# Attention scores on quarters of the matmul array, with the masked quarter of each tile left out

## The chip, the cores and the metric

One NeuronCore of a Trainium2 chip runs the whole program. The metric is the device time of one execution in microseconds (us), as a median over runs. TensorE (PE in the rows) does the matmuls and PEld is its weight load; VectorE (DVE), ScalarE (ACT) and GpSimd (POOL) work on elements; SyncE (SP) only issues DMA transfers.

## The reference, cut to what matters

```
scores = q @ k.T / sqrt(64)                     # batch 8, heads 8, seq 576, head_dim 64
D      = gamma[h] ** (i - j) where i >= j, else 0
attn   = (scores * D) @ v                       # -> x[4608, 512]
e      = argmax(x @ w_gate + modality_bias)     # one of 8 experts for each token
x      = gate * (relu(x @ w1[e]) @ w2[e])       # 512 -> 1024 -> 512
h      = x @ w_in                               # 512 -> 2048
out    = (h - tanh(h)) @ w_out                  # -> [4608, 512]
```

Only the first part, the attention with decay (a retention layer), is touched by the change. A score counts only where the key's position j is not after the query's position i.

## The kernel before, in words

The 4608 tokens of all eight batches stand in one row and are cut into 36 tiles of 128 tokens (`TL`, `NTILE`). A sequence has 576 tokens, which is 4.5 tiles, so the pattern of the sequences repeats every 9 tiles (`PERIOD`), and in every tile t with t % 9 == 4 one sequence ends and the next begins in the middle; the kernel calls it the mid tile. The decay is split into a factor for the query's position (`gx`, applied after the product with v) and one for the key's position (`vsc`, applied to v). What remains on the scores is a mask of ones and zeros.

The eight heads are four pairs p, each with two heads s = 0, 1. The work on a tile, by function:

- `scores(t)`: for each p and s one matmul of the 64 rows of head s (rows 0 to 63 or 64 to 127 of the array), all 128 columns (the key tokens) and 128 streamed query tokens, into a PSUM tile `sc` for each s (line 304). Two VectorE instructions of 128x512 elements then multiply `sc` by the mask into `a` (line 308). There are three `sc` buffers.
- `scaled(t)`: GpSimd makes `vs` = v times `vsc` (line 314).
- `attend(t)`: three groups of eight matmuls. `before()` adds what earlier tiles of the sequence give, from a running state: quarters of the array, 64 rows and 64 columns, 128 streamed tokens, or 64 in a mid tile (line 340). Line 348 adds the product of `a` and `vs`: 128 rows, halves of the columns. Line 363 brings the state forward from k and `vs`: 128 rows and halves of the columns, or in the mid tile the lower 64 rows alone. ScalarE copies the state to SBUF (line 367).
- `evac_x(t)`: VectorE multiplies the result `xp` by `gx` into `xt` (line 373). There is a single `xp` buffer, so the next tile's lines 340 and 348 wait for it.

The loop runs one tile ahead with the scores. Each pass t issues scores(t+1), attend(t), evac_x(t), scaled(t+4) and the loads of tile t+6. With every fourth tile the routing of a group of four tiles is woven in: `route_a` (line 404), `route_b` (transposes on line 413 and a chain of small VectorE instructions, lines 417 to 429) and `route_c` (small matmuls on lines 438 to 443, and a chain on lines 446 to 456). Each pass also transposes an older tile (line 471), which ScalarE scales by the gate and stores, and scatters token numbers by GpSimd (line 460). The order on every engine is the order of the program, written by hand. Where t % 9 is 0 there is nothing earlier in the sequence and `before()` does not run; in a mid tile it runs behind line 348; elsewhere it comes first, directly behind the scores of the next tile.

All these matmuls are in full float32, and each of them stands in the trace as two instructions (16 for eight matmuls), each with a weight load of its own.

Behind the attention come the experts (line 642 and lines 836 to 838) and the last two layers (line 642 and lines 910 to 912). The first unit of the experts starts on rows that GpSimd gathers (line 154) once tile 31's scatters have gone out; their transposes are on line 144.

## Time and profile before

| what | value |
|---|---|
| median of 3 runs (lowest to highest) | 1431.66 us (1431.45 to 1434.45) |
| the profiled execution, its own time | 1423.35 us |
| its span, from the first to the last instruction | 1421.6 us |
| granted TensorE clock, mean over the span | 0.994 |
| busy: PE, PEld, DVE, ACT, POOL | 98%, 85%, 73%, 48%, 16% |

The profiled execution is 8.3 us shorter than the median of the runs shown. A busy time is the union of an engine's instructions. Matmuls overlap each other in time, so the time that a group of them takes is read from where it starts to where the next group starts, and not from the durations. In the timeline a row gives the start, the time covered, engine, line, operation, tiles, shape and count; in brackets stands how long the engine had been idle, and what ended that.

### The profile page before, as it was taken

The page shows a single profiled execution, that of the slowest core. Times are in us where ns is not written, and L with a number is a line of the kernel's source. Part 1 is how long each engine was busy: PE and PEld are TensorE (multiplying, and loading weights), DVE is VectorE, ACT ScalarE, POOL GpSimd, SP SyncE. Part 2 cuts the span into 40 slices and gives each one's busy share as a digit, 9 for nine tenths or more (in the row PEclk, how much of TensorE's full clock was granted, in tenths as well). Part 3 has the DMA queues.
Part 4 walks back from the last instruction along what each step waited for, and adds up shares of the span by engine and source line. Part 5 has one row for each costly group of instructions (what it writes and reads, how often), then busy time and mean ns, then how long its engine had stood idle before and what let it go on. Part 6 is the DMA issues. An engine that isn't in the chain of part 4 may idle for free.

```text
span 1421.6 us, 22507 instructions
## 1 busy us (share of the span) xinstructions
PE 1392.0 (98%) x8427; PEld 1210.5 (85%) x8427; DVE 1044.5 (73%) x1761; ACT 682.9 (48%) x1269; POOL 220.8 (16%) x288
## 2 busy tenths in 40 slices
PE   7999999999999999989999999999999999999997
PEld 6888799999999999968888888888888888888885
DVE  3666678888888888557777777787777877778764
ACT  1233444444444444445555555555556555556553
POOL 3655420011111111100011100111001111011101
PEclk9999999999999999999999999999999999999999
DMA  9998533554754446253000000000000000000000
GB/s 355 407 335 304 192 131 124 135 135 136 228 116 79 90 121 162 71 165 127 30 30 30 30 1 30 30 30 30 1 30 30 30 30 0 30 30 1 30 1 30
DMA packets 65682, 138.71 MB, mean 98 GB/s; under 512 B 22480, under 2 KB 29328, under 8 KB 65568
## 3 DMA queue, kind: packets, MB, share of 16 engines
q1 hardware_dynamic: 49360, 96.15, 22.0%
q0 software_dynamic: 7904, 21.96, 4.6%
q10 hardware_dynamic: 8304, 19.11, 3.5%
q8 instruction: 68, 1.11, 0.3%
q14 instruction: 46, 0.38, 0.1%
HBM read 135.16 MB, written 39.80 MB: 123 GB/s over the span
## 4 chain that ended last, share of the span: by engine, by line
PE 50%; issue 5%; DVE 1%; POOL 0%; ACT 0%; POOLq 0%; DVEq 0%; ACTq 0%
PE hp L642 25%; PE acc L910 8%; PE acc L911 8%; PE acc L912 8%; POOL out_dram L935 0%; DVE xh L886 0%; DVE xl L893 0%; ACT xh L884 0%; DVE xl L895 0%; DVE xl L894 0%; DVE lo L889 0%; POOLq L963 0%; DVE xl L885 0%; POOL nopt L934 0%; ACT xh L883 0%
## 5 line engine op out<-in xcount | busy, mean ns | idle before, releaser
L883 ACT ACTIVATE xh<-hp 128x512 f32<-128x512 f32 x144 | 86.1, 598 | 329.9 <-PE hp L642 315.4
L910 PE MATMUL acc<-wout,hi 128*128 128x512 f32 x576 | 225.7, 392 | 5.1 <-ACT xh L883 5.1
L642 PE MATMUL hp<-yh,winh 128*128 128x512 f32 x576 | 226.4, 393 | 1.3 <-DVE epsb L939 1.3
L642 PE MATMUL hp<-yl,winh 128*128 128x512 f32 x576 | 226.2, 393 | 0.0
L642 PE MATMUL hp<-yh,winl 128*128 128x512 f32 x576 | 226.2, 393 | 0.0
L911 PE MATMUL acc<-wout,hi 128*128 128x512 f32 x576 | 225.6, 392 | 0.0
L912 PE MATMUL acc<-wout,lo 128*128 128x512 f32 x576 | 224.7, 390 | 0.0
L885 DVE TENSOR_TENSOR xl<-xh,hp 128x512 f32<-128x512 f32 x144 | 99.0, 687 | 167.7 <-ACT xh L884 167.7
L894 DVE SCALAR_TENSOR_TENSOR xl<-xh,xl 128x512 f32<-128x512 f32 x144 | 128.2, 890 | 15.4 <-DVE xl L893 0.5
L836 PE MATMUL acc<-hi,wh 128*128 128x400 f32 x384 | 136.9, 357 | 0.2
L910 PEld LDWEIGHTS acc<-wout,hi 128*128 128x128 f32 x576 | 108.6, 189 | 29.6 <-ACT xh L883 5.5
L642 PE MATMUL hp<-xl,wh 128*128 128x400 f32 x384 | 133.2, 347 | 0.1
L642 PE MATMUL hp<-xh,wl 128*128 128x400 f32 x384 | 133.0, 346 | 0.0
L642 PE MATMUL hp<-xh,wh 128*128 128x400 f32 x384 | 132.5, 345 | 0.2 <-ACT wh L711 0.2
L838 PE MATMUL acc<-hi,wl 128*128 128x400 f32 x384 | 132.6, 345 | 0.0
L837 PE MATMUL acc<-lo,wh 128*128 128x400 f32 x384 | 131.4, 342 | 0.0
L642 PEld LDWEIGHTS hp<-yh,winh 128*128 128x128 f32 x576 | 108.2, 188 | 25.7 <-PEq L857 1.6
L642 PEld LDWEIGHTS hp<-yh,winl 128*128 128x128 f32 x576 | 108.1, 188 | 24.6
L912 PEld LDWEIGHTS acc<-wout,lo 128*128 128x128 f32 x576 | 108.6, 189 | 23.9 <-DVE lo L889 0.4
L642 PEld LDWEIGHTS hp<-yl,winh 128*128 128x128 f32 x576 | 108.3, 188 | 23.9
L911 PEld LDWEIGHTS acc<-wout,hi 128*128 128x128 f32 x576 | 108.4, 188 | 23.1
L736 ACT ACTIVATE hi<-hp 128x400 fp32r<-128x400 f32 x96 | 48.4, 505 | 164.5 <-PE hp L642 164.5
(162 smaller groups left out, 2517.7 us busy)
## 6 DMA issues: line engine op xcount, KB each, us to landing
raw<-in_w_dram SPq DMA_DIRECT2D x91, 512.0 KB
qk<-in_qk_dram SPq DMA_DIRECT2D x36, 512.0 KB
vk<-in_vk_dram SPq DMA_DIRECT2D x35, 512.0 KB
y_d<-yo SPq DMA_DIRECT2D x12, 800.0 KB
yr<-y_d SPq DMA_DIRECT2D x9, 1024.0 KB
raw<-in_wo_dram SPq DMA_DIRECT2D x16, 512.0 KB
wo_d<-cv_em ACTq DMA_DIRECT2D x16, 512.0 KB
raw<-in_wi_dram SPq DMA_DIRECT2D x16, 512.0 KB
```

The lines of the kernel that those rows point to most:

```text
L642: nc.tensor.matmul(out=hp, lhsT=lhs, rhs=rhs, start=j == 0, stop=j == 3 * KD - 1)
L736: nc.scalar.activation(out=hi, in_=hp, func=ACTF.Relu)
L836: nc.tensor.matmul(out=o, lhsT=wh[:, cs], rhs=hi, start=first, stop=False)
L837: nc.tensor.matmul(out=o, lhsT=wh[:, cs], rhs=lo, start=False, stop=False)
L838: nc.tensor.matmul(out=o, lhsT=wl[:, cs], rhs=hi, start=False, stop=last)
L883: nc.scalar.activation(out=u, in_=hp, func=ACTF.Square)
L885: nc.vector.tensor_tensor(out=v, in0=u, in1=hp, op=ALU.mult)
L894: nc.vector.scalar_tensor_tensor(out=v, in0=s, scalar=SQ_C, in1=v, op0=ALU.add, op1=ALU.mult)
L910: nc.tensor.matmul(out=acc[s], lhsT=hi, rhs=wh, start=first, stop=False)
L911: nc.tensor.matmul(out=acc[s], lhsT=hi, rhs=wl, start=False, stop=False)
L912: nc.tensor.matmul(out=acc[s], lhsT=lo, rhs=wh, start=False, stop=last)
```

## The change

The scores of a pair are computed in quarters. For each p, the 64 key tokens of a half (kh = 0, 1) go to a block of 64 columns, c = kh XOR (p mod 2), so that every second pair has its key tokens swapped by halves. The upper half of the keys can only be seen by the upper half of the queries, so for kh = 1 only 64 query tokens are streamed. The other quarter of `a` is not computed. It is zeroed once at the start, in two `a` tiles that are used in turn. In place of two VectorE instructions for each tile there are six: for each s one of 128x256 elements for the upper queries, and one on each half of the partitions with 128 elements for the lower queries. The host swaps k, v, `vsc` and a second mask in the same way. As the halves of a mid tile then lie in different places for different pairs, its state product runs over all 128 rows, with a second `vs2` that is zero for the tokens of the older sequence.

```diff
 def _consts():
+    mask = np.stack([mask, np.roll(mask, 64, axis=0)], axis=2)
+    vsc = swapped(np.concatenate([vsc, vsc[:, PERIOD // 2:PERIOD // 2 + 1] * (j[:, :, None] >= 64)], axis=1)[None])[0]
...
-            mask = att.tile([128, 2, TL], F32, name="mask")
+            mask = att.tile([128, 2, 2, TL], F32, name="mask")
-            vsc = att.tile([128, PERIOD, H], F32, name="vsc")
+            vsc = att.tile([128, PERIOD + 1, H], F32, name="vsc")
+            weights = [att.tile([128, 2, H // 2, TL], F32, name=f"a{i}") for i in range(2)]
...
+            for a in weights:
+                nc.vector.memset(a, 0.0)
...
             def scores(t):
-                a = tmp.tile([128, 2, H // 2, TL], F32, name="a")
+                a = weights[t % 2]
                 for p in range(H // 2):
-                    for s in range(2):
-                        r64 = slice(64 * s, 64 * s + 64)
-                        nc.tensor.matmul(out=sc[s][:, p, :], lhsT=qk[r64, 1, p, :], rhs=qk[r64, 0, p, :],
-                                         start=True, stop=True, tile_position=(64 * s, 0))
+                    for kh in range(2):
+                        for s in range(2):
+                            r64, c = slice(64 * s, 64 * s + 64), kh ^ p % 2
+                            i = slice(64 * kh, TL)
+                            nc.tensor.matmul(out=sc[s][64 * c:64 * c + 64, p, i], lhsT=qk[r64, 1, p, 64 * kh:64 * kh + 64], rhs=qk[r64, 0, p, i],
+                                             start=True, stop=True, skip_group_check=True, tile_position=(64 * s, 64 * c))
...
                 for s in range(2):
-                    nc.vector.tensor_tensor(out=a[:, s], in0=sc[s], in1=mask[:, m:m + 1, :].to_broadcast([128, H // 2, TL]), op=ALU.mult)
+                    src = sc[s].rearrange("j (b q) i -> j b q i", q=2)
+                    dst = a[:, s].rearrange("j (b q) i -> j b q i", q=2)
+                    nc.vector.tensor_tensor(out=dst[:, :, :, half], in0=src[:, :, :, half],
+                                            in1=mask[:, m, :, half].unsqueeze(1).to_broadcast([128, 2, 2, TL // 2]), op=ALU.mult)
+                    for q in range(2):
+                        r64 = slice(64 * q, 64 * q + 64)
+                        nc.vector.tensor_tensor(out=dst[r64, :, q, 0:TL // 2], in0=src[r64, :, q, 0:TL // 2],
+                                                in1=mask[r64, m, q:q + 1, 0:TL // 2].to_broadcast([64, 2, TL // 2]), op=ALU.mult)
...
             def scaled(t):
+                if t % PERIOD == PERIOD // 2:
+                    v2_t[t] = tmp.tile([128, H, D], F32, name="vs2", bufs=1)
+                    nc.gpsimd.tensor_tensor(
+                        out=v2_t[t], in0=vk[:, 0].rearrange("p (h d) -> p h d", h=H),
+                        in1=vsc[:, PERIOD].unsqueeze(2).to_broadcast([128, H, D]), op=ALU.mult)
...
             def attend(t):
-                    k0 = TL // 2 if mid_t else 0
+                    vs = v2_t.pop(t) if mid_t else vs
-                            nc.tensor.matmul(out=st[64 * s:64 * s + 64, p, :], lhsT=vk[k0:TL, 1, h * D:(h + 1) * D],
-                                             rhs=vs[k0:TL, h], start=first and p == 0, stop=True, skip_group_check=True,
-                                             tile_position=(k0, 64 * s))
+                            nc.tensor.matmul(out=st[64 * s:64 * s + 64, p, :], lhsT=vk[:, 1, h * D:(h + 1) * D],
+                                             rhs=vs[:, h], start=first and p == 0, stop=True, skip_group_check=True,
+                                             tile_position=(0, 64 * s))
```

## Rows read from the trace of the kernel before

**Rows 1.** Stretches: length, busy time (count) of each engine, clock, DMA share, GB/s.

```profile
50.00:100.00 50.00, 49.93 (x855) 40.88 (x855) 33.44 (x83) 15.27 (x31) 29.21 (x42) 1.00 1.00 369
175.00:1421.00 1246.00, 1230.51 (x5900) 1077.04 (x5898) 937.82 (x1494) 634.80 (x1172) 134.53 (x157) 1.00 0.23 67
```

**Rows 2.** Timeline of PE from 30 to 34 us, with a mid tile.

```profile
30.67 1.09 PE L348 MATMUL xp<-a,vs 128*64 128x128 f32 x16
31.69 0.46 PE L340 MATMUL xp<-qk,state 64*64 64x64 f32 x16
31.98 0.64 PE L363 MATMUL st<-vs,vk 64*64 64x64 f32 x16
32.55 1.06 PE L404 MATMUL m<-xt,wg 128*32 128x512 f32 x8
33.80 0.94 PE L304 MATMUL sc<-qk 64*128 64x128 f32 x12 [0.19 <-DMA qk<-in_qk_dram]
```

**Rows 3.** Timeline of PE and DVE around one pass of the loop.

```profile
106.06 1.16 PE L304 MATMUL sc<-qk 64*128 64x128 f32 x16
...
107.15 0.67 PE L340 MATMUL xp<-qk,state 64*64 64x128 f32 x16
...
107.58 1.25 DVE L308 TENSOR_TENSOR a<-sc,mask 128x512 f32<-128x512 f32 x2
107.74 1.09 PE L348 MATMUL xp<-a,vs 128*64 128x128 f32 x16
...
108.67 0.63 PE L363 MATMUL st<-vs,vk 128*64 128x64 f32 x16
108.89 0.69 DVE L373 TENSOR_TENSOR xt<-xp,gx 128x512 f32<-128x512 f32 x1
...
109.82 1.16 PE L304 MATMUL sc<-qk 64*128 64x128 f32 x16
110.91 0.67 PE L340 MATMUL xp<-qk,state 64*64 64x128 f32 x16
```

**Rows 4.** Timeline of PE cut to 0.05 and 0.04 us: what had started.

```profile
106.06 0.38 PE L304 MATMUL sc<-qk 64*128 64x128 f32 x2
...
107.15 0.34 PE L340 MATMUL xp<-qk,state 64*64 64x128 f32 x4
```

**Rows 5.** Groups by line, 0 to 170 us: busy us, mean ns, idle before and releasers.

```profile
L308 DVE TENSOR_TENSOR a<-sc,mask 128x512 f32<-128x512 f32 x72 | 46.1, 681 | 41.7 <-PE sc L304 41.6
L314 POOL TENSOR_TENSOR vs<-vk,vsc 128x512 f32<-128x512 f32 x36 | 37.3, 1036 | 66.0 <-DMA vk<-in_vk_dram 28.8 <-PE st L363 28.6 <-PE xp L348 3.9
...
L447 DVE TENSOR_TENSOR rk<-rk,oh_all 128x32 f32<-128x32 f32 x8 | 3.6, 447 | 0.3
...
L146 DVE TENSOR_TENSOR xl<-xp,xh 128x64 fp32r<-128x64 f32 x1 | 0.2, 223 | 0.2 <-ACT xh L145 0.2
```

**Rows 6.** Timeline of DVE: its first instruction, and a routing chain.

```profile
7.73 1.29 DVE L308 TENSOR_TENSOR a<-sc,mask 128x512 f32<-128x512 f32 x2 [7.73 <-PE sc L304]
...
103.64 1.28 DVE L308 TENSOR_TENSOR a<-sc,mask 128x512 f32<-128x512 f32 x2
...
105.68 0.19 DVE L446 TENSOR_TENSOR rk<-m,ecap 128x32 f32<-128x32 f32 x1
105.90 0.71 DVE L447 TENSOR_TENSOR rk<-rk,oh_all 128x32 f32<-128x32 f32 x1
```

**Rows 7.** DMA issues, 0 to 170 us.

```profile
mask<-in_mask_dram ACTq DMA_DIRECT2D x1, 128.0 KB
```

**Rows 8.** Timeline at the end of the attention: POOL, then PE.

```profile
141.82 1.03 POOL L314 TENSOR_TENSOR vs<-vk,vsc 128x512 f32<-128x512 f32 x1 [1.91 <-PE st L363]
...
151.93 0.99 POOL L154 DMA_INDIRECT vk<-x_d,idt  x1 [4.08 <-issue]
...
160.37 0.39 PE L144 MATMUL xp<-ident,vk 16*128 16x16 f32 x4 [0.92 <-DMA vk<-x_d,idt]
```

**Rows 9.** Stretch behind it, columns as in group 1.

```profile
161.50:165.50 4.00, 3.92 (x12) 3.46 (x13) 1.29 (x2) 0.55 (x2) 0.35 (x2) 0.57 0.04 11
```

More of the change, by code (lines that the diff above doesn't have):

```diff
@@ L50, with swapped @@
 SQ_A, SQ_B, SQ_C, SQ_R = 0.1408476404964593, -0.007447476355480239, 0.1278048703835037, 2.6070111457436247
+def swapped(a):
+    a = np.array(a)
+    ax = [n for n, w in enumerate(a.shape) if w == H and n >= 2][-1]
+    v = np.moveaxis(a, ax, 0)
+    for h in range(H):
+        if h // 2 % 2:
+            v[h] = np.roll(v[h], 64, axis=1)
+    return a
 def _consts():
@@ L80, in tok @@
     def tok(a):
-        return a.transpose(0, 2, 1, 3).reshape(NTILE, TL, DM)
+        return swapped(a.transpose(0, 2, 1, 3).reshape(NTILE, TL, H, D)).reshape(NTILE, TL, DM)
     w1 = inputs["moe_w1"][:, FEATURES].reshape(E, KD, 128, F1, 128).transpose(0, 3, 2, 1, 4).reshape(E, F1, 128, DM)
@@ L291 @@
             nc.gpsimd.memset(cum[:, 0], 0.0)
-            a_t, v_t, s_t, x_ps = {}, {}, {}, {}
+            a_t, v_t, v2_t, s_t, x_ps = {}, {}, {}, {}, {}
             xt = {}
@@ L298, in scores @@
                 qk, vk = gt[t]
-                a = tmp.tile([128, 2, H // 2, TL], F32, name="a")
+                a = weights[t % 2]
                 sc = [ps_sc.tile([128, H // 2, TL], F32, name="sc") for _ in range(2)]
                 for p in range(H // 2):
-                    for s in range(2):
-                        r64 = slice(64 * s, 64 * s + 64)
-                        nc.tensor.matmul(out=sc[s][:, p, :], lhsT=qk[r64, 1, p, :], rhs=qk[r64, 0, p, :],
-                                         start=True, stop=True, tile_position=(64 * s, 0))
+                    for kh in range(2):
[4 more added lines that the diff above has]
+                                             start=True, stop=True, skip_group_check=True, tile_position=(64 * s, 64 * c))
                 m = int(t % PERIOD == PERIOD // 2)
+                half = slice(TL // 2, TL)
                 for s in range(2):
-                    nc.vector.tensor_tensor(out=a[:, s], in0=sc[s], in1=mask[:, m:m + 1, :].to_broadcast([128, H // 2, TL]), op=ALU.mult)
+                    src = sc[s].rearrange("j (b q) i -> j b q i", q=2)
[6 more added lines that the diff above has]
+                                                in1=mask[r64, m, q:q + 1, 0:TL // 2].to_broadcast([64, 2, TL // 2]), op=ALU.mult)
                 a_t[t] = a
```

## The prediction, made before the changed kernel ran

> **What bounds the kernel now.** I read the stretches first, because the change touches only the attention. From 175 us to the end PE is busy 1230.5 of 1246 us [rows 1], so whatever the attention ends earlier or later moves the end by as much. Inside the attention PE is busy 49.9 of 50 us, DVE 33.4 and POOL 29.2, and the DMA share is 1.00 [rows 1]. A full DMA share could mean that the loads set the pace, so I went to the timeline of PE next, looking for waits. It shows one for qk at 33.80, where tile 6's scores begin [rows 2]. Behind it the groups of a pass follow each other without a marked wait [rows 3]: PE's program order sets the pace from there to about 156 us, over tiles 6 to 35, and the loads run ahead. Before tile 6 what PE saves is lost to the next load.
>
> Durations of single matmuls say little, as they overlap; I take start to start. In a pass [rows 3] the scores take 1.09 us (106.06 to 107.15), line 340 0.59, line 348 0.93.
>
> **Scores in quarters.** The nearest rows are line 340's, which already run on quarters. Four of its matmuls had started within 0.04 us of the group's start, two of the scores' [rows 4], so the four quarters run at once. Each quarter does 4 of the 16 instructions. Let w be the first weight load, a an instruction with 128 streamed tokens, b one with 64. Line 348, with 8 instructions in each half and the same shape behind it: w + 8a = 0.93. Line 340 in a mid tile, again with the same shape behind it: w + 4b = 0.29 [rows 2]. Neither gives w alone; between 0 and 0.1 us it hardly matters, and I take 0.05. Then a = 0.11 and b = 0.06. Line 340 with 128 tokens and another shape behind it takes 0.59 = w + 4a + d, so a change of array shape costs d = 0.10; in the mid tile line 348 into line 340 takes 1.02 against 0.93, which says 0.09 [rows 2, 3].
>
> In the new scores every quarter gets four long and four short instructions (p even and p odd exchange the blocks): 0.05 + 4 x 0.11 + 4 x 0.06 = 0.73 (0.70 to 0.76 over the range of w). What it saves depends on what follows:
> - line 340, now of the same shape, so that d goes and its first weights load under the scores: 1.09 - 0.73 + 0.05 = 0.41. Of the passes 5 to 34, which hold scores 6 to 35, 24 are such.
> - line 348, where t % 9 is 0: 1.09 - 0.73 - 0.10 = 0.26, three times.
> - the mid tiles: the same 0.26, but line 363 now runs on 128 rows behind line 340's quarters, a new change of shape, 0.10: 0.16, three times. Its own instructions stay 16, with 64 streamed tokens.
>
> Sum for PE: 24 x 0.41 + 3 x 0.26 + 3 x 0.16 = 11.1 us.
>
> **The mask multiplies.** Two DVE instructions become six, and on half of the partitions I count an instruction by its elements in one partition, so that the six still have 1024 to go through. Line 308 takes 0.68 for 512 elements, line 146 0.22 for 64 [rows 5]: 0.154 + 0.00103 n, so 0.42 for 256 and 0.285 for 128, and 1.98 for the six end to end. Neighbours overlap: two of 0.68 take 1.25 [rows 3], 0.1 less. The low bound is an overlap at all six joints, 1.4 us to the next instruction against 1.2 now. The high bound is a wait for the one before at each, 0.03 more than end to end, as in a routing chain (105.68 + 0.19 to 105.90 [rows 6]): 2.15. Three of the six, and the next tile's first, begin on other partitions than the one before, and no row shows such neighbours overlapping; I take an overlap at the two other joints alone, 1.8.
>
> [...]
>
> Is DVE covered? With 33.4 of 50 us it has room on average, but it works in order and line 373 stands behind the multiplies. The tightest place is the routing: from 103.64 on, DVE works nearly without a pause up to line 373 at 108.89, which ends at 109.58 [rows 3, 6]. It frees the only `xp` buffer, and the next line 340 starts at 110.91: 1.33 us of room. The change takes from both sides. PE passes three scores between the start of that chain and 110.91, 3 x 0.41 = 1.23 less. DVE has two multiplies in it, 2 x 0.6, of which its short waits absorb some 0.3: 0.9 more. So PE stalls 0.8 there. In that chain line 447 took 0.71; its mean is 0.45 [rows 5, 6], so an average chain is 0.25 shorter: 0.55 for each of seven such groups, 3.9 us. Bounds: at 1.4 nothing is left of the stall; at 2.15 DVE has 2 x 0.35 more, so 1.25 x 7 = 8.8.
>
> **The rest.** The mask grows by 128 KB [rows 7]. The first tiles wait on loads; at 369 GB/s [rows 1] 131 KB are 0.4 us, which I count as a loss; nothing, if they arrive beside a wait for something else. The zeroing runs on DVE, which does nothing before 7.73 [rows 6]; two tiles of 1024 elements are about 2.2 us at line 308's slope, hidden, and without that cover 2.2 once. `vs2` is four more POOL instructions of 1.04 [rows 5] on an engine idle for 66 us before that line alone: nothing; uncovered, 4.2. What waits behind them on POOL are scatters, needed only at the end. There the gathers form a chain that PE does not pace: the last `vs` waits for line 363 of tile 31 until 141.82, and 18.5 us later PE waits 0.92 for the fourth gather [rows 8]. Three scores lie in that time, so 1.2 us of PE's gain would become waiting. But tile 31 is a mid tile; its `vs` is now free after line 348, 0.9 to 1.1 us sooner. Loss: 0.2.
>
> Sum: 11.1 - 3.9 - 0.4 - 0.2 = 6.6 us gained. On the profiled execution's 1423.35 that is 1416.8; on the median of the runs, which lies 8.3 above it, **1425.1 us**.
>
> **Rivals.**
> - DVE waits nowhere: gain 10.5, so 1421.2. For it speaks that line 308's pairs overlap [rows 3]; against it, the joints that change partitions.
> - Each of the six waits for the one before: 11.1 - 8.8 - 0.6 = 1.7, so 1430.0. This would need dependences between writes that do not overlap.
> - The loads set the pace: a tile moves 1.05 MB in and 0.26 MB out, at 369 GB/s [rows 1] 3.55 us, against 4.0 a tile now (tile 6's scores at 33.80, tile 24's at 106.06 [rows 2, 3]) and 3.65 with PE's whole gain. They would still be covered; if the qk wait at 33.80 [rows 2] came back for some tiles, the gain might halve: 1428.
> - Slower: a quarter's second pass holds up the matmuls behind it, so that matmuls start in program order. A pair is then three slots of a and two of b, 0.11 x 2 + 0.06 x 2 = 0.34 from pair to pair, 0.05 + 4 x 0.34 = 1.41 a tile. By the three cases above, 24 x 0.27 + 3 x 0.42 + 3 x 0.52 = 9.3 are lost, with the mask 9.7: 1441. It decides from a group of 1.14 us on, where the first case gains nothing. Against it: four starts in 0.04 us [rows 4], and 8 matmuls of line 340 in 0.59, where this order would need 0.9.
>
> [...]
>
> **How the numbers follow.** Forecast 0.50; no DVE wait 0.22; chained DVE 0.10; loads 0.08; program order 0.06; the change not doing what it says (quarters that do not run at once with unequal lengths, about no change) 0.04. The clock adds a little: behind the attention it was granted at 0.57 over 4 us [rows 9], after PE had waited 0.92 [rows 8]. [...] Range 1419.5 to 1430: from no DVE wait with a lucky clock to the chained case; outside lie program order, no change, half of the chained case and the tails. The forecast's own is 1422.5 to 1427.5. A change of 0.2%, 2.9 us, is about what a measurement can tell from none: faster 0.76 (forecast 0.47, no wait 0.22, half of the loads', some of the chained), same 0.17 (most of the chained, the rest of the loads', no change), slower 0.07.
>
> **What would show it.** Right: the scores take 0.73 from start to start, line 340 0.55 behind them; six DVE instructions take about 1.8; line 340 waits for line 373 once in four tiles; the attention ends some 7 us sooner and nothing behind it changes its length. Wrong: scores at 1.2 or more, waits for qk beyond tile 7, or an `a` that comes so late that line 348 waits for it.

## The result, and the profile after

The changed kernel took 1443.28 us (median of 7 runs, 1439.68 to 1445.33) where the kernel before, run beside it, took 1433.27 (1431.05 to 1435.96): a ratio of 1.0069, 95% interval 1.0057 to 1.0082. It is 0.7% slower; the forecast was 1425.1, in the range 1419.5 to 1430.0, so both the sign and the range were wrong. Two repetitions gave 1.0065 (1.0051 to 1.0079) and 1.0062 (1.0049 to 1.0075).

One thing has to be known to read the numbers: the kernel before had a median of 1433 us on some occasions and of 1424 on others, so kernels are compared by their ratio to the kernel before on the same occasion, and only such traces side by side. The trace before [rows 1 to 9] is of the faster kind, the first trace after of the slower. Their spans, 1421.6 and 1443.6 us, differ by 22 us, of which some 10 to 14 are the occasion's: the kernel before, traced on an occasion of the slower kind (e11 below), starts its first expert unit 10.6 us later than in the trace before and has a span of 1435.3.

The waits of PE from 0 to 200 us, changed kernel (in us in total, times, longest). The lines have moved: 304 is now 325, 308 is 332 (128x256) and 336 (64x128), 340 is 374, 348 is 382, 363 is 397, 373 is 407, 446 is 480, 642 is 676.

```profile
PE sc L325 <- DMA qk<-in_qk_dram: 11.8, 3, 6.3
PE xp L374 <- issue: 5.6, 11, 1.2
PE hp L676 <- ACT wh L745: 4.7, 1, 4.7
PE xp L374 <- DVE rk L480: 3.3, 4, 1.7
PE xp L374 <- DVE xt L407: 2.0, 5, 0.8
PE m L472 <- DVE oh_all L463: 1.2, 2, 0.9
```

In the trace before the same list has 10.1 us for qk, and the next largest entry is 0.9. Three kinds of wait are new or have grown: "issue" (PE waits for nothing that the trace shows), DVE, and one of 4.7 us for the weights of the first expert unit. The stretches (columns as in [rows 1]) show the same: between 50 and 100 us PE is busy 46.0 us where it was 49.9, and DVE 36.7 where it was 33.4. Behind the attention PE is as full as before, apart from the 4.7 us.

```profile
50.00:100.00 50.00, 46.01 (x978) 37.23 (x975) 36.69 (x123) 13.99 (x28) 28.13 (x40) 0.97 0.93 338
175.00:1443.00 1268.00, 1246.87 (x5994) 1090.84 (x5991) 948.97 (x1522) 645.01 (x1192) 138.36 (x163) 0.99 0.23 69
```

Timeline of PE in the changed kernel: an undisturbed pass, to be read against [rows 3], and a disturbed one.

```profile
75.06 0.90 PE L325 MATMUL sc<-qk 64*64 64x128 f32 x32
75.78 0.62 PE L374 MATMUL xp<-qk,state 64*64 64x128 f32 x16
76.33 1.09 PE L382 MATMUL xp<-a,vs 128*64 128x128 f32 x16
...
87.07 0.90 PE L325 MATMUL sc<-qk 64*64 64x128 f32 x32
87.79 0.40 PE L374 MATMUL xp<-qk,state 64*64 64x128 f32 x5
89.43 0.65 PE L374 MATMUL xp<-qk,state 64*64 64x128 f32 x11 [1.24 <-issue]
90.01 1.09 PE L382 MATMUL xp<-a,vs 128*64 128x128 f32 x16
```

From start to start the scores take 0.72 us (75.06 to 75.78) and line 374 behind them 0.55, as forecast. But line 374 at 87.79 stops after 5 of its 16 instructions, with no semaphore to wait for, and goes on 1.24 us later. DVE's timeline has the six instructions at 1.91 us to the next one (100.75 to 102.66):

```profile
100.75 0.42 DVE L332 TENSOR_TENSOR a<-sc,mask 128x256 f32<-128x256 f32 x1 [0.31 <-PE sc L325]
101.09 0.58 DVE L336 TENSOR_TENSOR a<-sc,mask 64x128 f32<-64x128 f32 x2
101.70 0.43 DVE L332 TENSOR_TENSOR a<-sc,mask 128x256 f32<-128x256 f32 x1
102.04 0.58 DVE L336 TENSOR_TENSOR a<-sc,mask 64x128 f32<-64x128 f32 x2
102.66 0.69 DVE L407 TENSOR_TENSOR xt<-xp,gx 128x512 f32<-128x512 f32 x1
```

Part of what the list of waits calls "issue" or puts down to the routing chain (`rk`) is a wait for line 407, which frees the only `xp` buffer. In the timelines of DVE and of PE's weight loads, line 407 ends at 62.46, and line 374's loads start 0.12 us behind it. The same 0.12 stands at nine of the passes between 43 and 141 us.

```profile
61.77 0.69 DVE L407 TENSOR_TENSOR xt<-xp,gx 128x512 f32<-128x512 f32 x1
62.58 0.76 PEld L374 LDWEIGHTS xp<-qk,state 64*64 64x64 f32 x16 [0.94 <-issue]
```

Behind this wait, and one of 0.87 us just before it, PE's granted clock, 1.00 from 60 to 62 us, was 0.63 for 2 us and then 0.52 (0.50 from 63 to 65); in the kernel before it was 1.00 from 60 to 80 us. The two waits in PE's timeline, and the two stretches:

```profile
60.01 0.19 PE L472 MATMUL m<-oh_all,ltri 128*128 128x32 bf16 x1 [0.87 <-DVE oh_all L463]
...
62.61 1.13 PE L374 MATMUL xp<-qk,state 64*64 64x128 f32 x16 [0.78 <-DVE rk L480]
...
62.00:64.00 2.00, 1.39 (x20) 1.09 (x22) 1.83 (x10) 0.09 (x1) 1.01 (x1) 0.63 1.02 414
64.00:66.00 2.00, 2.00 (x28) 2.00 (x26) 1.83 (x7) 0.60 (x1) 0.00 (x0) 0.52 0.99 305
```

And at the end of the attention, timelines of PE and of SP's transfers: the first weight loads go out at 178.05, and PE stands for 4.66 us.

```profile
176.81 0.66 PE L505 MATMUL m<-ident,xt 128*128 128x128 f32 x4
182.12 0.70 PE L676 MATMUL hp<-xh,wh 128*128 128x400 f32 x1 [4.66 <-ACT wh L745]
...
178.05 1.53 SPq L738 DMA_DIRECT2D raw<-in_w_dram  x3
```

In the trace before they go out from 150.82 on, 10.8 us ahead of the first unit:

```profile
150.82 6.74 SPq L704 DMA_DIRECT2D raw<-in_w_dram  x3
...
161.58 0.47 PE L642 MATMUL hp<-xh,wh 128*128 128x400 f32 x1 [0.23 <-ACT wh L711]
```

To put one number on PE's disturbances, I took each group of matmuls that starts between 43 and 141 us, from its start to the start of the next group, and summed what it takes over the shortest of its kind (same line, count and line behind it). This "time over the shortest" is 1.0 us in the kernel before (on either kind of occasion) and 16.0 in the changed kernel. Of the 16.0, 6.7 us are waits of lines 374 and 472 for DVE, 3.6 stand at three pauses like the one at 87.79, 1.6 in groups under the lower clock, and the other 4.1 in small pieces that I did not assign. The measure is somewhat low: a group whose count is unusual, because some of its instructions are missing or out of order in the trace, has no other to be compared with.

### The profile page after: what moved, and what is told of

The parts are those of the page before. It is cut to its first block, busy times and chain, and to the rows that moved or that the text cites. A ratio compares the mean times of both kernels' runs of the same rounds, so it can differ in the third digit from the quotient of the medians.

```text
span 1443.6 us, 23851 instructions
## 1 busy us (share of the span) xinstructions
PE 1395.0 (97%) x9003; PEld 1209.9 (84%) x9003; DVE 1064.6 (74%) x1907; ACT 683.2 (47%) x1269; POOL 225.0 (16%) x292
## 3 DMA queue, kind: packets, MB, share of 16 engines
q8 instruction: 72, 1.18, 0.3%
## 4 chain that ended last, share of the span: by engine, by line
PE 49%; issue 5%; POOL 0%; DMA 0%; DVE 0%; ACT 0%; POOLq 0%; DVEq 0%; ACTq 0%
PE hp L676 25%; PE acc L944 8%; PE acc L945 8%; PE acc L946 8%; DMA wout<-wo_d 0%; POOL out_dram L969 0%; DVE xh L920 0%; ACT xh L918 0%; POOLq L997 0%; DVE xl L929 0%; DVE xl L919 0%; DVE xl L928 0%; POOL nopt L968 0%; DVE xl L927 0%; DVE lo L923 0%
## 5 line engine op out<-in xcount | busy, mean ns | idle before, releaser
L746 DVE TENSOR_TENSOR wl<-raw,wh 128x512 fp32r<-128x512 f32 x192 | 124.5, 688 | 4.3 <-ACT wh L745 4.3
```

Of the source, the lines that this page charges most:

```text
L746: nc.vector.tensor_tensor(out=wl, in0=r, in1=wh.bitcast(F32), op=ALU.subtract)
```

## The experiments

**Addresses, DVE and instructions, first round.** In the changed kernel the load buffers lie 9,248 bytes higher in each partition (the zeroed tiles, mask, `vsc`), and the first weight loads, at fixed addresses, now lie over gathered rows that are read until the attention ends.

e1_layout, from the changed kernel:

```diff
-            mask = att.tile([128, 2, 2, TL], F32, name="mask")
+            pad = att.tile([128, 2 * TL + PERIOD * H], F32, name="pad")
-            vsc = att.tile([128, PERIOD + 1, H], F32, name="vsc")
-            weights = [att.tile([128, 2, H // 2, TL], F32, name=f"a{i}") for i in range(2)]
...
+            vs_bufs = [tmp.tile([128, H, D], F32, name=f"vs_{i}", bufs=1) for i in range(4)]
+            weights = [tmp.tile([128, 2, H // 2, TL], F32, name=f"a{i}", bufs=1) for i in range(2)]
+            mask = tmp.tile([128, 2, 2, TL], F32, name="mask", bufs=1)
+            vsc = tmp.tile([128, PERIOD + 1, H], F32, name="vsc", bufs=1)
```

> The changed kernel with its new buffers (the two zeroed score tiles, the larger mask and scale tables) moved behind the buffers of the loads, so that every buffer that the kernel before had lies at its old address. Nothing else changes. Theory 'addresses': in the changed kernel the first three weight loads of the first expert unit lie over buffers of gathered rows that are read until 177 us, so they start at 178 us and PE waits 4.66 us for them in one piece. Here they should start near 150 us, that wait should fall under 0.5 us, and the time should be some 4.4 us below the changed kernel's 1443.3: about 1438.9. Rival 'the loads are hidden by something else': the wait moves to another cause at the same place and the time stays within 1 us of 1443.3.

e2_two_multiplies, in addition:

```diff
-                sc = [ps_sc.tile([128, H // 2, TL], F32, name="sc") for _ in range(2)]
+                sc = [scores_ps[(2 * t + s) % 3] for s in range(2)]
...
-                    nc.vector.tensor_tensor(out=dst[:, :, :, half], in0=src[:, :, :, half],
-                                            in1=mask[:, m, :, half].unsqueeze(1).to_broadcast([128, 2, 2, TL // 2]), op=ALU.mult)
...
+                    nc.vector.tensor_tensor(out=a[:, s].rearrange("j (b q) i -> j b q i", q=2), in0=sc[s].rearrange("j (b q) i -> j b q i", q=2),
+                                            in1=mask[:, m].unsqueeze(1).to_broadcast([128, 2, 2, TL]), op=ALU.mult)
```

> As e1_layout, but the masked multiply is two DVE instructions of 512 elements a tile again, as in the kernel before: the quarter that is not computed is zeroed once in three fixed accumulators and multiplied by a mask of 0. PE's instructions are those of the changed kernel. Theory 'DVE': the six instructions cost what they hold up, PE's waits for DVE in the attention (more than 6 us in the changed kernel's trace) fall to those of the kernel before, and with PE's own gain of 11 us the time comes out below the kernel before: 1422 to 1426. Theory 'instructions': PE also pauses, with no releaser, for some 10 us in all because its instructions arrive late; the quarters' matmuls are still there, so the pauses stay at 5 to 10 us and the time comes out at 1428 to 1434.

e3_split, from the kernel before:

```diff
...
-                        nc.tensor.matmul(out=sc[s][:, p, :], lhsT=qk[r64, 1, p, :], rhs=qk[r64, 0, p, :],
...
+                    for i in (slice(0, 64), slice(64, TL)):
...
+                            nc.tensor.matmul(out=sc[s][:, p, i], lhsT=qk[r64, 1, p, :], rhs=qk[r64, 0, p, i],
```

> The kernel before, with each of the eight score matmuls of a tile split in two by columns (64 each), the same number of matmul instructions as the changed kernel has, on the old shape of the array, with the old mask multiplies and the old addresses. Theory 'instructions': pauses of PE without a releaser appear between matmuls of one group, at the same place in each block of 256 instruction records as in the changed kernel (about 193 behind its start), 3 to 10 us in all, and the time rises by that, to 1436 or more, beside whatever the group's own length adds. Rival 'shape': only quarters or the DVE queue bring the pauses, none of over 0.3 us appears here, and the time changes only by the group's own length (16 shorter passes a half instead of 8, estimated at no more than 0.1 us a tile, 3.6 us).

e0_before_again is the kernel before, unedited.

> The kernel before once more, unchanged, for a second trace, since its profiled execution lay 8 us under its median. If its time varies with pauses of PE for instructions, a trace at the median shows some us of them inside the attention; if it varies elsewhere, the attention ends at 161.6 us again and the difference lies behind it.

| run | us | ratio (95%) | time over the shortest |
|---|---|---|---|
| e1_layout | 1429.71 | 1.0035 (1.0022 to 1.0048) | 10.5 |
| e2_two_multiplies | 1423.12 | 0.9997 (0.9989 to 1.0006) | 8.5 |
| e3_split | 1449.05 | 1.0180 (1.0167 to 1.0193) | 0.8 |
| e0_before_again | 1423.81 | | 1.0 |

The kernel before was at 1423.54 here. Taking the DVE instructions back gave 6.6 us (e1 to e2), but e2, with PE's shorter scores and the old mask multiplies, only came back to the kernel before, which fits the theory of instructions and not that of DVE alone. (The profiled execution of e2 was its longest, 4.7 us over the median, so a median execution may have fewer pauses than this trace.) Its pauses move from line to line. PE's groups in e2 from 50 to 100 us (busy us, mean ns, idle before and releasers):

```profile
L377 PE MATMUL xp<-a,vs 128*64 128x128 f32 x207 | 14.4, 279 | 1.3 <-issue 1.3
L327 PE MATMUL sc<-qk 64*64 64x128 f32 (+1 forms) x384 | 11.5, 251 | 1.1 <-issue 1.1
L500 PE MATMUL m<-ident,xt 128*128 128x128 f32 x48 | 7.6, 282 | 0.0
L392 PE MATMUL st<-vs,vk 128*64 128x64 f32 x176 | 7.4, 223 | 0.0
L369 PE MATMUL xp<-qk,state 64*64 64x128 f32 (+1 forms) x160 | 6.6, 268 | 1.1 <-issue 0.8 <-ACT state L396 0.3
```

What they have in common is their place in PE's stream of instructions. If all of PE's records (matmuls, weight loads, semaphore waits) are counted in order of start, eight pauses of 0.78 to 1.69 us in e2, 9.5 us in all, stand at record 193, or one beside it, of a block of 256; in e1_layout six of 0.38 to 1.51 us, all at 193. (The expectation of e4 below counts ten in e2; two of those stand at other records, one of them a wait for DVE.) The trace also has the transfers that bring the instructions: a queue of its own moved 72 packets, 1.18 MB, over the changed kernel's span, 16,384 bytes each, and 18,153 records make 71 blocks of 256. Block by block, from the traces' records (us; the sixth column is when PE comes to record 193, the last how long it stands there):

```
kernel  block  PE at 193 of   its transfer starts  takes   PE at 193 of   pause there
               the block ahead   behind that               this block
before    10      87.73             3.13           0.89       94.67          0.00
          15     124.34             3.14           0.96      131.99          0.10
e2        10      74.41             4.47           0.96       79.80          1.37
          11      81.17             4.04           0.98       86.34          1.12
          15     104.82             3.62           1.02      109.69          1.13
          16     110.82             5.55           0.93      116.96          1.69
e4        10      69.88             0.07           1.26       75.22          0.00
          16     102.41             0.79           2.39      108.56          0.03
```

Before, PE needs 6.3 to 8.5 us for 256 records (blocks 3 to 18), and a transfer that is in after 4 us is in time. In e2 PE would need some 5 to 6.7, the transfers of the four rows start 3.6 to 5.6 us behind and take 1, and PE goes on 1.3 to 1.4 us after they have landed. (e4 follows.) The same holds in every trace of this case. In their blocks 3 to 20, as far as 141 us, 47 have a pause of over 0.3 us at record 193, and each time PE goes on 1.2 to 1.5 us after that block's transfer has landed; in the 272 others PE comes to record 193 no sooner than 1.2 us after the landing. From block 5 to block 19, 11 of e2's 15 blocks stand within 1.6 us of their landing; in the trace before none is closer than 2.9. So these pauses are waits for the instruction transfer.

e3_split missed both of its theories: no pauses, but the time rose by 25.5 us. Its timeline of PE shows why; the scores take 1.93 us (102.38 to 104.31) instead of 1.09.

```profile
102.38 2.00 PE L305 MATMUL sc<-qk 64*128 64x64 f32 x32
104.31 0.67 PE L341 MATMUL xp<-qk,state 64*64 64x128 f32 x16
```

On 128 columns an instruction that streams 64 tokens, with its weight load, takes nearly as long as one that streams 128 (0.060 us against 0.068); I had assumed half. 0.84 us on some 30 tiles are the 25. So e3 has the changed kernel's instruction count at a slower pace (6.5 to 8.6 us a block), and says only that the count alone brings no pause. As for the base, e0's first unit starts at 161.4 us, as in the trace before (161.6), so the 8 us between that execution and the median lie in the occasion.

**Are the transfers late because the rings are full?** By full rings I mean no more than that loads keep the DMA engines busy nearly all the time (a DMA share near 1.00). e4_two_relief (from e2_two_multiplies), e5_before_relief (from the kernel before) and e7_six_relief (from e1_layout) have the same edit, which leaves out the loads of v and k by token from tile 6 on:

```diff
-                vk = gld.tile([128, 2, DM], F32, name="vk")
+                if t < AHEAD:
+                    vk_bufs.append(gld.tile([128, 2, DM], F32, name="vk"))
...
+                vk = vk_bufs[t % AHEAD]
```

> As e2_two_multiplies, but from tile 6 on the values and keys by token (vk, 512 KB a tile) are not loaded: the tile uses those of an earlier one in the same buffer. That leaves out part of the input, so tokens may be routed differently; e5_before_relief does the same to the kernel before. About half of the loads of the attention are gone. In e2's trace PE stood still ten times for 0.8 to 1.7 us, 11 us in all, each time at record 193 of a block of 256 of its instructions, while that block's instruction transfer was late: it started 3 to 5.5 us after the PE had reached the same point of the block before, and took 1 us. Theory 'instructions behind full rings': the transfer is late because the rings are full of loads; with half of the loads it starts within 2 us, the pauses fall under 2 us in all, and the time comes out 8 to 11 us under e5_before_relief. Rival 'the rate itself': PE can't have 256 instructions in less than 6 us whatever the rings carry; the pauses stay at 8 us or more and the time is that of e5_before_relief within 2 us.

> The kernel before with the same loads of vk left out from tile 6 on (its tokens may be routed differently too). It has no such pauses, and beyond tile 6 it does not wait for loads: both theories expect its time within 3 us of the kernel before, and the attention to end at 158 to 162 us. It is the base for e4_two_relief and e7_six_relief.

> As e1_layout (six mask instructions, old addresses), with the loads of vk left out from tile 6 on as in e4_two_relief. With no pauses for instructions, what the six DVE instructions cost by themselves stands between this and e4_two_relief: by the prediction's step 3.9 us (bounds 0 and 8.8); e1_layout and e2_two_multiplies stood 6.6 us apart with the pauses in both. Expected: 4 to 8 us above e4_two_relief, with waits of line 376 for DVE once in four tiles. If the two are within 1.5 us, the 6.6 us were not DVE's own but came with the pauses.

| run | us | time over the shortest |
|---|---|---|
| e5_before_relief | 1428.07 (1427.53 to 1429.59) | 0.9 |
| e4_two_relief | 1414.68 (1413.98 to 1416.43) | 1.0 |
| e7_six_relief | 1422.56 (1421.37 to 1426.71) | 7.3 |

With half of the loads gone the quarters gain 13.4 us (e5 to e4), where with all loads they gained 0.4 (e2). Some 3.3 of the 13.4 are not the quarters' but a longer wait at e5's first unit, whose weight loads go out at 159.85 instead of 150.82. PE's timelines there, e5 and then e4:

```profile
159.64 0.66 PE L474 MATMUL m<-ident,xt 128*128 128x128 f32 x4
163.81 0.70 PE L645 MATMUL hp<-xh,wh 128*128 128x400 f32 x1 [3.51 <-ACT wh L714]
...
151.53 0.66 PE L503 MATMUL m<-ident,xt 128*128 128x128 f32 x4
152.42 0.45 PE L674 MATMUL hp<-xh,wh 128*128 128x400 f32 x1 [0.23 <-ACT wh L743]
```

The last matmul ahead of the first unit ends at 160.3 us in e5 and at 152.2 in e4, 8.1 us apart; with all loads it ended at 161.4 in the trace before and at 161.7 in e2. From the scores of tile 9 on, behind e4's last pause, PE takes 115.2 us to that end in e5 and 106.2 in e4: 9.0 us are what the quarters give it there. PE's groups in e4, 50 to 100 us, have no idle time before them:

```profile
L380 PE MATMUL xp<-a,vs 128*64 128x128 f32 x224 | 15.3, 279 | 0.0
L330 PE MATMUL sc<-qk 64*64 64x128 f32 x448 | 12.6, 250 | 0.0
L395 PE MATMUL st<-vs,vk 128*64 128x64 f32 x208 | 8.3, 223 | 0.0
```

The transfers start within 1.7 us of record 193 of the block ahead from block 5 on, and DMA's share from 50 to 100 us is 0.67, against 0.99 in e2. The rival of a fixed rate falls: PE had 256 records in 4.6 to 6.5 us without a pause. e5 is 4.3 us over the kernel before, a little outside its expectation, by the wait at its first unit. The six DVE instructions cost 7.9 us without any pauses (e4 to e7).

**Fewer quarters.** Three kernels with two multiplies ask for fewer instructions. e6_every_second, from e2_two_multiplies (the keys of odd pairs lie swapped by halves in memory, so both forms can use them):

```diff
-                    for kh in range(2):
+                    for kh in range(2 if t % 2 else 1):
+                            j = slice(64 * c, 64 * c + 64) if t % 2 else slice(0, TL)
```

> As e2_two_multiplies with the full loads, but only the odd tiles compute their scores on quarters, with 16 matmuls; the even tiles use the eight full matmuls of the kernel before (the keys of every second pair are laid down swapped by halves for both). Nothing is left out. Theory 'instructions behind full rings': PE asks for 162 instruction records a tile instead of 178, so most pauses go (under 4 us in all) while half of PE's gain, some 5 to 6 us, stays: 3 to 6 us under the kernel before. Rival 'each quarter matmul costs what it saves': half of e2's nothing is nothing, the time is that of the kernel before within 1.5 us.

e8_odd_from_6 and e9_two_thirds take `t >= 6 and t % 2` and `t >= 6 and t % 3` instead, and load half of the mask later.

> As e6_every_second, but quarters only in the odd tiles from 7 on (the first tiles wait for loads anyway), and the second half of the mask, which tile 4 needs first, is loaded after the first four tiles. Nothing is left out. Theory 'instructions behind full rings': no pause of over 0.5 us at record 193; half of PE's gain over the tiles 7 to 35 stays: 15 tiles of 0.37, 5.6 us, less what waits take. Expected 3 to 5 us under the kernel before, ratio 0.9965 to 0.998; e6_every_second came to 0.9987, having lost 1.3 us to the loads at the start and 1.4 us to one wait for ACT.

> As e8_odd_from_6, but quarters in two tiles of three from 7 on (167 records a tile on average where e8 has 162 and e2_two_multiplies 178). Theory 'instructions behind full rings': pauses come back in part, 2 to 5 us in all, so the further gain of 1.8 us is used up and the time is within 1.5 us of e8_odd_from_6. Rival 'no limit before 178': 2 us under e8_odd_from_6.

e6 gave 1422.14, ratio 0.9987 (0.9978 to 0.9996), time over the shortest 3.5 with one pause of 0.43 us at record 193: the direction expected, but half of the size. e8 gave 1434.80, 1.0008 (0.9998 to 1.0017), time over the shortest 6.2, e9 1433.75, 0.9996 (0.9987 to 1.0005) and 11.6, on an occasion with the kernel before at 1433.68. The pauses at record 193 grow with the quarters as expected (none of over 0.3 us in e8, two of 2.0 us together in e9); the gain expected of e8 did not show. (The profiled execution of e9 was 7 us over its median.) No version beat the kernel before on both kinds of occasion.

Much of the time over the shortest in these three is another wait, in the pass near 54 us, for ACT's copy of the state: 1.6 us in e6, 0.6 in e8, 3.6 in e9. ACT's order is the program's, and a store that it issues goes out late: in e16 (below), ready at 51.99, it goes out at 56.70, and the copy stands behind it (timelines of ACT and PE):

```profile
51.30 0.69 ACT L507 ACTIVATE xo<-m,gate 128x512 f32<-128x512 f32 x1
56.70 0.33 ACTq L508 DMA_DIRECT2D x_d<-xo  x1
57.06 0.37 ACT L398 COPY state<-st 128x256 f32<-128x256 f32 x1 [5.07 <-DMA vk<-in_vk_dram]
...
54.49 0.94 PE L329 MATMUL sc<-qk 64*64 64x128 f32 x32
57.49 0.67 PE L371 MATMUL xp<-qk,state 64*64 64x128 f32 x16 [2.06 <-ACT state L398]
```

In the kernel before a store there is 3.2 us late too, but PE, which is slower, hardly waits for the copy (0.3 us); with half of the loads gone (e4) one goes out at once, ready at 50.70 and out at 50.73. So the loads seem to hold up ACT's stores as well; no run takes this apart.

**The occasion and the addresses, again.** e10_changed_again and e12_changed_third are the changed kernel, e11_before_third is the kernel before, e13_layout_again and e14_two_again are e1_layout and e2_two_multiplies, all unedited.

> The changed kernel itself once more, for its ratio and trace beside those of e1_layout, which was run on another occasion. Theory 'addresses': PE waits 4 to 5 us for the first weight loads again, and the ratio to the kernel before is 1.006 to 1.008 against 1.0035 for e1_layout. The first trace of the changed kernel also shows nine us of single matmuls about 0.7 us apart between 152 and 165 us, which no other trace shows; if they belong to the kernel they come again, if to that one execution they do not, and the attention then ends near 172 us rather than 182.

> The kernel before a third time. The medians of the kernel before were 1433.5 us on the occasions of both runs of the changed kernel and 1423.6 on those of e1 to e7. All four traces of the slower occasions (changed kernel twice, e8, e9) show some 5 to 9 us between 140 and 165 us in which PE's instructions come about 0.7 us apart, and none of the faster occasions does. If those 10 us belong to the occasion and not to a change, then this run shows them too if it comes out near 1433, and does not if it comes out near 1423.

> The changed kernel for a comparison with the next two on one occasion. Expected 1.005 to 1.008 of the kernel before.

> e1_layout on one occasion with the changed kernel. Theory 'addresses': 3 to 5 us under e12_changed_third. Rival: the 1.0035 of e1_layout against 1.0065 came from the occasions; the two are within 1.5 us of each other.

> e2_two_multiplies on one occasion with the two above: 5 to 8 us under e13_layout_again, as before, which the six DVE instructions cost, and within 2 us of the kernel before.

e10 gave 1443.33 (1.0065), e12 1442.91 (1.0062), e13 1441.06 (1.0043, 1.0029 to 1.0057), e14 1435.39 (1.0012, 1.0002 to 1.0021), e11 1437.01 in its one run. The single matmuls 0.7 us apart came again in e10, and the kernel before has such a stretch on this occasion too (timeline of PE in e11; before, these groups ran through in 0.92 and 0.57 us):

```profile
145.83 0.49 PE L348 MATMUL xp<-a,vs 128*64 128x128 f32 x2
146.73 0.38 PE L348 MATMUL xp<-a,vs 128*64 128x128 f32 x2 [0.41 <-issue]
147.47 0.35 PE L363 MATMUL st<-vs,vk 128*64 128x64 f32 x4 [0.35 <-issue]
148.91 0.58 PE L363 MATMUL st<-vs,vk 128*64 128x64 f32 x12 [1.09 <-issue]
```

The scores of its tile 33 start within 0.2 us of the trace before, at 143.43 against 143.25 us, its first unit at 172.2 instead of 161.6, after a wait of 1.49 us. So that stretch belongs to the occasion, and the changed kernel ends its attention at 179 to 183 us, 7 to 11 later than the kernel before there. My guess of 172 in e10 was wrong, as I took the base for 161.6.

e1_layout had not done what it was meant to. In the kernel before, the gathered rows lie at 80,928 and 85,024 bytes in a partition; in e1 they got the buffers at 89,120 and 93,216, and the first weight load, at 96,000, overlaps the latter. It went out at 163.6 us, and PE waited 1.9 us. e15_free moves `gx` and the score tiles up, so that nothing lies from 96,000 to 108,288; e16_two_free and e17_odd_free do that to e2_two_multiplies and e8_odd_from_6.

```diff
-            gx = att.tile([128, PERIOD, H // 2, TL], F32, name="gx")
+            pad = tmp.tile([128, 432 + 3 * 1024], F32, name="pad", bufs=1)
...
+            gx = tmp.tile([128, PERIOD, H // 2, TL], F32, name="gx", bufs=1)
```

> As e1_layout, but the attention's buffers are placed so that nothing lies at all where the first three weight loads of the first expert unit go. e1_layout did not undo the addresses as it was meant to: its gathered rows lie in other load buffers than those of the kernel before, under the first of the three loads, so that load still waited for the gather, until 163.6 us, and PE 1.9 us for it. Theory 'addresses': the loads start with the others of their queue, right behind the table of the chosen expert's rows (about 152 us, some 10 us before PE needs them), PE's wait at the first unit falls to 0.5 us, and the time is 1.5 to 4 us under e1_layout's ratios of 1.0035 and 1.0043, so 1.001 to 1.003. Rival 'hidden': the earlier loads take ring time from the attention, and the ratio stays at 1.0035 to 1.0045.

> The same placing with two multiplies (e2_two_multiplies). Quarters, the mask as before, free addresses: what is left of the change's loss are the pauses for instructions. Expected 4 to 8 us under e15_free and 1.5 to 3 us under e2_two_multiplies' ratios of 0.9997 and 1.0012: 0.997 to 0.999.

> The same placing with quarters in the odd tiles from 7 on (e8_odd_from_6, which came to 1.0008 with a wait of 2.5 us for the weights). Expected 2 us less: 0.998 to 0.9995.

e15 gave 1440.30, 1.0046 (1.0030 to 1.0063), e16 1435.11, 1.0006 (0.9996 to 1.0016), e17 1434.25, 1.0008 (0.9997 to 1.0019). SP's transfers and PE at the first unit, in e15:

```profile
152.92 0.42 SPq L164 DMA_DIRECT2D idt<-slot_d  x1
153.54 1.41 SPq L741 DMA_DIRECT2D raw<-in_w_dram  x3
...
176.66 0.70 PE L679 MATMUL hp<-xh,wh 128*128 128x400 f32 x1 [1.52 <-ACT wh L748]
```

The loads go out 23 us ahead, and the wait falls from 4.66 to 1.52 us, about what it is in the kernel before on this kind of occasion (e11):

```profile
172.22 0.45 PE L642 MATMUL hp<-xh,wh 128*128 128x400 f32 x1 [1.49 <-ACT wh L711]
```

The time falls by 0.0019, 2.7 us, against the mean of the changed kernel's three ratios (1.0065), but the intervals are some 2 us either way, and e15, expected at 1.001 to 1.003, is no faster than e1 and e13, as its rival said. So the addresses cost about 3 us in the trace; the times neither contradict nor prove it. Six instructions against two cost 5.2 us once more (e15 to e16). e16 and e17 missed their expectations by 2 to 5 us.

e16 has the change's whole gain for PE, without the six multiplies and the addresses, and is no faster than the kernel before. But late instructions are not all of that: of its time over the shortest, 11.9 us, pauses at record 193 are 1.2 (e14: 3.5 of 10.9). The wait for ACT above is 2.3, the groups behind it, at a granted clock of 0.68 and then 0.50 from 58 to 62 us, are 1.5, and waits for DVE are 1.3; the other half are pieces of under 0.8 us, most without a releaser, that I could not assign. e17 loses 6.0 us with no pause of over 0.3 us at record 193 at all.

## Why the prediction was wrong

**What was right.** The scores at 0.73 (0.72), line 340 behind them at 0.55 (0.55), the price of a change of shape at 0.10 (scores into line 382 take 0.83 instead of 0.72: 0.11), and the quarters running at once: the rival of program order names almost the measured time, but its scores at 1.41 did not come, so that is chance. PE's gain came too: from tile 9 on, where the prediction's cases add up to 9.9 us, e4 is 9.0 us shorter than e5. The loads' own waits stayed at the first tiles (11.8 against 10.1 us).

**The step that failed: "PE's program order sets the pace from there to about 156 us, over tiles 6 to 35, and the loads run ahead."** On it rests that the 11.1 us for PE come off the time, less 3.9 for DVE, 0.4 for the mask and 0.2 for the gathers. In the changed kernel PE's time over the shortest rose by 15.0 us instead, more than PE gained: by 6.7 for DVE, 3.6 for late instructions, 1.6 for the clock and some 3 that I did not assign.

The change doubles the scores' instructions, 32 for 16, each with its weight load. These 32 more records a tile have to come in by transfers of 256 records, while the loads keep the DMA engines busy ([rows 1]: share 1.00). I had read that row, and asked of the full rings only whether data would be late. The rival "the loads set the pace" was costed by waits for qk, which did not come; what came late were PE's instructions, a term that the sum does not have. On the faster occasion it is nearly as large as the gain: in e2, which has the whole change for PE and ends at 0.9997, the pauses at record 193 come to 8.0 us between 43 and 141 us. With 16 records less a tile on average (e6) the pauses nearly go, with half of the loads (e4) they go. On the slower occasion, where the result was measured, it is smaller, 3.6 us in the changed kernel and 1.2 to 3.5 in e16 and e14, and yet these two end at 1.0006 and 1.0012: what else takes the gain there is shown only in part.

**The DVE term was mis-sized.** "3.9 us, bounds 0 and 8.8" came out at 5.2 to 6.6 by the times of runs with all loads (e15 to e16, e1 to e2), at 7.9 without the pauses (e7 to e4), and at 6.7 in the changed kernel's trace. The mechanism was the one predicted: line 374 waits for line 407, which stands behind the multiplies and the routing chain. The single wait was about right (0.64 us on average, 0.55 forecast), but it comes at nine of some 24 passes, not "once in four tiles"; 0.9 us more is line 472, waiting for the chain itself. The six take 1.91 instead of 1.8 us. The halves of the partitions follow end to end (0.58 for two of 0.284), while the 128x256 instruction lets its neighbour start after 0.34 of its 0.42: these rows have an overlap at two of the six joints, as the prediction chose. The clock, which the prediction counted only as a possible gain behind the attention, cost 1.6 us inside it, after two of these waits. The range begins 1.7 us under the rival without a DVE wait, for the clock, and no run shows that term: in the traces the clock is 0.50 from 162 to 165 us before, and 0.50 again from 182 to 185 in the changed kernel, behind its wait of 4.66 us.

**"Nothing behind it changes its length"** (said of the attention) failed at its first step: the wait at the first unit, 0.23 us in the trace before and 1.49 in e11, is 3.9 to 4.7 in the changed kernel's three traces, as the new buffers moved the old ones under the weight loads behind. The prediction has no word on where the buffers lie.

The sum on one occasion, in us against the kernel before: quarters with two multiplies and free addresses +0.9 (e16), six multiplies +5.2 (e15 to e16), addresses +2.7 (changed kernel to e15), together +8.8, against 9 to 10 measured. These are steps along one chain of kernels, so that they add up proves nothing by itself. The first number hides PE's gain of some 9 and disturbances of the same size, of which the late instructions are a part.

**What stays open.** How the 0.7 us steps of the slower occasions arise; they are in both kernels, and from the scores of tile 32 to the end of the attention e11 takes 31.9 us and the changed kernel 30.8, so they explain no difference. What takes PE's gain there besides DVE, ACT and the late instructions: e8 and e17 keep none of theirs, while e6 kept 1.6 us on the faster occasion. That the transfers queue behind the loads' packets is inferred from taking loads away (starts at most 1.7 us behind in e4, up to 5.6 in e2); the order in the rings is not shown.

## What to carry to other kernels

Count the instructions that a change adds as well as what they stream: at a DMA share of 0.99, the transfers of PE's instructions started 1.2 to 5.6 us behind PE in e2, mostly over 3, and this kernel, which would use up a block in some 5 to 6.7 us, lost again most of what shorter matmuls give (8.0 us of pauses). A pause that no semaphore explains is worth counting in records: if it comes at the same place in every block, lay the landing of the instruction transfer beside it. Where only one buffer stands between two engines, count in how many passes the wait comes, as well as its length. And a buffer that is added moves the others: look where the first loads of the next stage will land, and what is still read there.

## What the runs showed of the hardware that was not expected

- PE's instructions came in transfers of 16,384 bytes, 256 records (72 transfers for 18,153 records in the changed kernel). With the rings full (share 0.99) they started 1.2 to 5.6 us, mostly over 3, behind the point where PE passes record 193 of the block ahead in e2; with half of the loads (share 0.67) 1.7 us at most (e4, from block 5 on). PE did not pass record 193 before 1.2 us after the block's transfer had landed: 47 pauses and 272 blocks without one, in 20 traces.
- On 64 rows and 128 columns a matmul instruction that streams 64 tokens, with a weight load of its own, took nearly as long as one that streams 128: 1.93 us for 32 against 1.09 for 16 (e3). On 64 x 64 quarters the shorter stream did pay (0.72 us for 32, half of them with 64 tokens).
- PE's granted clock fell from 1.00 to 0.50 for some 3 us after waits of 0.87 and 0.78 us close together (changed kernel, 60 to 66 us), and to 0.50 after one of 2.06 (e16, 55 to 62 us).
- On the slower occasions PE's instructions came about 0.7 us apart for several us between 144 and 165 us, in the kernel before too (e11), with DMA's share at 0.29 to 0.33 there in e8, so that full rings do not explain it.
